# Loads, masks, units and means of a gated-convolution and MLP kernel put in another order

## The chip, the cores and the metric

The kernel runs on one core of one Trainium2 chip. The metric is the time of one execution on the device in microseconds (us). Traces come from the hardware profiler, one execution each. The engines are TensorE (PE for matmuls, PEld for its weight loads), VectorE (DVE), ScalarE (ACT) and GpSimd (POOL); SyncE (SP) issues most DMAs, and ACT's queue issues some.

## What is computed

```python
def _A_ref(q, k, v, shift_k, ssm_k, ssm_D):      # q = layernorm(x)
    ...
        k_shift = k_shift + k_pad[:, t:t + S, :] * shift_k[:, ks - 1 - t][None, None, :]
    kv = k_shift * v
    ...  # FFTs of length L = 2 * S along the sequence
    y_f = kv_f * kf_f[None, :, :, :]
    y = (irfft2 of y_f).astype(jnp.bfloat16)[:, 0, :S, :]
    y = y + kv * ssm_D[None, None, :]
    return q * y

x = A_q
h = x + _A_ref(_layernorm(x, axis=-1), A_k, A_v, A_shift_k, A_ssm_k, A_ssm_D)
h2 = h + _B_ref(_layernorm(h, axis=-1), B_w1, B_w2)     # relu(h @ w1) @ w2
```

S is 2048, D is 512, the shift filter has 4 taps, the MLP is 1376 wide, inputs are bf16. So: four taps along the sequence give kv, a causal convolution as long as the sequence (with ssm_k, one filter per channel) gives y, the gate multiplies it by the normalised x, and an MLP follows.

## The kernel before

The convolution is done as a transform in two matmul stages on each side, a product, and an inverse in two stages. No planner orders the work: it is written out by hand, and each engine runs its instructions in the order of the text. A wait is made only for data or for a buffer that must come free.

- **Loads.** ssm_k comes in eight pieces of 256 KB into kfl: group rg (32 partitions) and half d. `load_rows` (L104) issues both halves of a group. SP issues groups 0 and 2 at once; ACT issues wsh (the taps, L126), drow (ssm_D, L127), group 1 (L128), then the two sines of f1f and group 3 (L222). SP goes on with k (`load_k`, DMA transposes, L140), v (`load_v`, L112), the first quarter of x (`load_x0`, into qn0) and w1 (`load_w1`, L154). There are four buffers for k; two of them first hold tables of turns (tb, L138).
- **Tables.** Integer turns (multiply-add, then a bit mask; `_turns`, L182, on DVE) go through a sine on ACT (`_sin`). f1f, 128x64, becomes f1w for stage 1: a bf16 high part and a low part (f1hi, f1lo, L242 to L244), copied by POOL to the quadrants of f1w (`paired`, L253), the rest zero. `spikes` (L248) does the same to drow for drow2. The large table tab has index i (which 16 of the k1) and b; `turns2`, `sines2` and `negated` (POOL, L275) fill it. Second-stage units read its entries 0 to 2 in the K-side; the product also reads entry 3. `inverse_turns` (POOL, L291) prepares the tables of the inverse, and `diagonals` (POOL, L261) makes wdiag, the taps' weights.
- **Stage 1 of ssm_k.** `s1(gb, engs)` (L423, `stage1`, L343), gb from 0 to 7: 32 matmuls, and four that add drow2, into two PSUM tiles, then two copies to a1k by the engines named ("AD" is ACT and DVE). All PSUM tiles are of two banks; there are four, in two pools taken in turn (`bank2`, L322).
- **Taps.** `tap(u, eng)`, u from 0 to 7: 16 matmuls, one PSUM tile, one copy to ksh.
- **Second-stage units.** `second_k(kp, eng)` (L396), kp from 0 to 15: 8 matmuls from tab and a1k, one PSUM tile, one copy back into a1k.
- **Rows.** `row(q)` (L466, `to_rows`, L329): 16 transposes of ksh by PE, then DVE multiplies by v into xfl. x is normalised on the way: bn_stats, `moments` (L444), `norm_rows` (L451, DVE).
- **Stage 1 of x.** Eight blocks of `stage1` on xfl into a1x (L547). After blocks 0 and 2 stand `column_means` (L404, PE and an ACT copy) and `center` (L412, POOL, 2 of 4 each), which take the column means off w1.
- **Products.** `product(kp, pool)` (L571), kp from 0 to 15: u2 and u1, 8 matmuls and one PSUM tile each; DVE multiplies u2 by a1k into a1x; u1's product goes to DVE, or by an ACT copy (usb) to POOL for ten of the sixteen. `steps` adds three ACT table operations (`last_table`).
- Behind them come the inverse (DVE transposes, L619), the gate, and the MLP with the output. None of that is edited.

Of the kernel before, what the change touches and what calls it, by code (L numbers as in the profile page):

```python
# [9 lines left out]
ALU = mybir.AluOpType  # L10
BF16 = mybir.dt.bfloat16
F32 = mybir.dt.float32
# [3 lines left out]
P = 128  # L16
# [39 lines left out]
def kernel(  # L56
# [37 lines left out]
    def first_channel(rg, d):  # L94
        return 128 * rg + 64 * (d ^ (rg % 2))
# [5 lines left out]

    kfl = front.tile([P, 64, 2, 64], BF16, name="kfl")

    def load_rows(eng, rg):  # L104
        for d in range(2):
            src = bass.AP(tensor=A_ssm_k.tensor, offset=A_ssm_k.offset + S * first_channel(rg, d), ap=[[64, 32], [S, 64], [1, 64]])
            eng.dma_start(out=kfl[32 * rg:32 * rg + 32, :, d, :], in_=src)


    vfl = front.tile([P, 64, P], BF16, name="vfl")  # L110

    def load_v(r):  # L112
        for d in range(2) if r % 2 else (0,):
            n = 64 if r % 2 else P
            src = bass.AP(tensor=A_v.tensor, offset=A_v.offset + first_channel(r, d), ap=[[64 * D, 32], [D, 64], [1, n]])
            nc.sync.dma_start(out=vfl[32 * r:32 * r + 32, :, 64 * d:64 * d + n], in_=src)

    zero = consts.tile([P, 512], BF16, name="zero")
    nc.vector.memset(zero[:], 0.0)
# [2 lines left out]
    nc.vector.memset(drow[:], 0.0)  # L122

    drow2 = consts.tile([P, 2, 64], BF16, name="drow2")
    nc.vector.memset(drow2[:], 0.0)
    nc.scalar.dma_start(out=wsh[:], in_=A_shift_k.rearrange("(r p) j -> p r j", p=P))  # L126
    nc.scalar.dma_start(out=drow[0:P:16, :], in_=A_ssm_D.rearrange("(r g) -> r g", g=64))  # L127
    load_rows(nc.scalar, 1)  # L128
    for rg in (0, 2):
        load_rows(nc.sync, rg)  # L130
    CH = 512
    kT = {}

    def chunk(name):
        return front.tile([P, DC, CH + 16], BF16, tag="kT", name=name, bufs=4)


    tb = [chunk(f"tb{b}")[:].rearrange("p c t -> p (c t)").bitcast(I32)[:, 0:1024].rearrange("p (a b) -> p a b", b=64) for b in range(2)]  # L138

    def load_k(c):  # L140
        kT[c] = chunk("kT")
        if c == 0:
            nc.vector.memset(kT[c][:, :, 0:16], 0.0)
            nc.sync.dma_start_transpose(out=kT[c][:, :, 16:CH + 16], in_=k_d[0:CH, :])
        else:
            nc.sync.dma_start_transpose(out=kT[c][:], in_=k_d[CH * c - 16:CH * c + CH, :])
# [30 lines left out]
    def _sin(out, turns, M, neg=False):  # L177

        nc.scalar.activation(out=out, in_=turns, func=ACT.Sin, scale=(-TURN if neg else TURN) / M,
                             bias=(pbias if neg else nbias)[:])  # L180

    def _turns(out, r, col, M, add):  # L182

        nc.vector.tensor_scalar(out=out, in0=r, scalar1=col, scalar2=add, op0=ALU.mult, op1=ALU.add)
        nc.vector.tensor_single_scalar(out=out, in_=out, scalar=M - 1, op=ALU.bitwise_and)
# [33 lines left out]
    f1f = early.tile([P, 64], F32, name="f1f")  # L219
    _sin(f1f[:, 0:32], t1[:, 0:32], 128)  # L220
    _sin(f1f[:, 32:64], t1[:, 32:64], 128, neg=True)
    load_rows(nc.scalar, 3)  # L222
    o2 = consts.tile([P, 2, 2], F32, name="o2")
    for i in range(2):
        for b in range(2):
            nc.vector.tensor_scalar(out=o2[:, i, b:b + 1], in0=n2c[:], scalar1=32.0 * i, scalar2=4096.0 + 2048.0 * b,
                                    op0=ALU.mult, op1=ALU.add)

    def turns2(i, b):
        ta = tb[b] if i else early.tile([P, 16, 64], I32, tag="ta", name="ta", bufs=2)[:]  # L230
        _turns(ta, r2, n2c[:], 8192, o2[:, i, b:b + 1])
        return ta

    ta00 = turns2(0, 0)
    ta01 = turns2(0, 1)
    f1hi = consts.tile([P, 64], BF16, name="f1hi")
    f1lo = consts.tile([P, 64], BF16, name="f1lo")
    f1d = early.tile([P, 64], F32, name="f1d")


    tab = tabp.tile([P, 32, 4, 64], F32R, name="tab")
    nc.vector.tensor_copy(out=f1hi[:], in_=f1f[:])  # L242
    nc.vector.tensor_tensor(out=f1d[:], in0=f1f[:], in1=f1hi[:], op=ALU.subtract)
    nc.vector.tensor_copy(out=f1lo[:], in_=f1d[:])  # L244

    f1w = consts.tile([P, 2, 2, 64], BF16, name="f1w")

    def spikes():  # L248
        for rg in range(DC):
            q = slice(32 * rg, 32 * rg + 32)  # L250
            nc.vector.tensor_copy(out=drow2[q, rg % 2, :], in_=drow[q, :])  # L251

    def paired():  # L253
        nc.gpsimd.memset(f1w[:], 0.0)
        for rg in range(DC):
            for i, f in enumerate((f1hi, f1lo)):
                nc.gpsimd.tensor_copy(out=f1w[32 * rg:32 * rg + 32, i, rg % 2, :], in_=f[32 * rg:32 * rg + 32, :])  # L257

    wdiag = rows.tile([P, DC, KS, 64], BF16, name="wdiag")

    def diagonals():  # L261
        ident2 = early.tile([P, 64], BF16, name="ident2")
        for e in range(2):
            p = slice(64 * e, 64 * e + 64)
            nc.gpsimd.tensor_copy(out=ident2[p, :], in_=ident[p, p])
        for w in range(DC):
            nc.gpsimd.tensor_tensor(out=wdiag[:, w, :, :], in0=ident2[:].unsqueeze(1).to_broadcast([P, KS, 64]),
                                    in1=wsh[:, w, :].unsqueeze(2).to_broadcast([P, KS, 64]), op=ALU.mult)

    wm = rows.tile([P, 4, 344], F32, name="wm")  # L270

    def sines2(i, b, ta):
        _sin(tab[:, 16 * i:16 * i + 16, b, :], ta, 8192)

    def negated(i):  # L275
        nc.gpsimd.tensor_single_scalar(out=tab[:, 8 * i:8 * i + 8, 2:4, :], in_=tab[:, 8 * i:8 * i + 8, 0:2, :].bitcast(F32),
                                       scalar=-1.0, op=ALU.mult)


# [116 lines left out]
    def second_k(kp, eng):  # L396
        ps = bank2("ps2k")
        second(ps, a1k, kp, 0)
        copy(eng, spot(a1k, kp), ps[:])
# [12 lines left out]
    def center(n):  # L412
        fs = slice(n * FS, (n + 1) * FS)
        nc.gpsimd.tensor_tensor(out=w1[:, :, fs], in0=w1[:, :, fs], in1=wm[:, n, :].unsqueeze(1).to_broadcast([P, DC, FS]),  # L414
                                op=ALU.subtract)


    def warm(n, data=zero[:], lhsT=None):
        ps = bank2("warm")
        for i in range(n):  # L420
            nc.tensor.matmul(out=ps[:, i % 2, :], lhsT=data[:, 0:P] if lhsT is None else lhsT, rhs=data, start=True, stop=True)  # L421
# [26 lines left out]
        nc.gpsimd.tensor_single_scalar(out=r[:, ts, :], in_=mv[:, ts, 1:2], scalar=EPS, op=ALU.add)  # L448
        nc.gpsimd.tensor_tensor(out=r[:, ts, :], in0=r[:, ts, :], in1=mhalf[:, 0:4].unsqueeze(2), op=ALU.pow)

    def norm_rows(q, out, src):  # L451
        for i in range(4):
            t = 4 * q + i
            nc.vector.tensor_scalar(out=out[:, i, :], in0=src[:, i, :], scalar1=mv1[:, t, 0:1],
                                    scalar2=rstd1[:, t, :], op0=ALU.subtract, op1=ALU.mult)

    xfl = None
# [14 lines left out]
    def seconds(kps, engs):  # L472
        for kp, eng in zip(kps, engs):
            second_k(kp, eng)

    load_k(0)
    load_k(1)
    spikes()
    sines2(0, 0, ta00)
    ta10 = turns2(1, 0)  # L480
    sines2(0, 1, ta01)
    ta11 = turns2(1, 1)
    diagonals()
    paired()
    negated(0)
    negated(1)
    sines2(1, 0, ta10)
    sines2(1, 1, ta11)
    load_k(2)
    load_k(3)  # L490
    load_v(0)
    load_v(2)
    load_x0()
    load_v(1)
    load_v(3)
    load_w1()
    negated(2)
    negated(3)
    inverse_turns()
    warm(13, lhsT=wdiag[:, 0, 0:2].rearrange("p j g -> p (j g)"))  # L500
    s1(0, "AD")
    s1(1, "AD")
    s1(2, "AD")
    tap(0, "A")
    s1(3, "AD")
    s1(4, "AD")
    tap(1, "D")
    s1(5, "AD")
    s1(6, "AD")
    s1(7, "AD")  # L510
    tap(2, "A")
    second_k(0, "A")
    second_k(1, "D")
    second_k(2, "A")
    tap(3, "A")
    second_k(3, "D")
    second_k(4, "A")
    tap(4, "A")
    second_k(5, "D")
    pairs_pool()  # L520
    second_k(6, "A")
    tap(5, "D")
    nc.vector.bn_stats(out=st[:, 0, :], in_=qn0[:, 0, :])
    second_k(7, "A")
    tap(6, "A")
    nc.vector.bn_stats(out=st[:, 1, :], in_=qn0[:, 1, :])
    second_k(8, "A")
    tap(7, "D")
    nc.vector.bn_stats(out=st[:, 2, :], in_=qn0[:, 2, :])
    nc.vector.bn_stats(out=st[:, 3, :], in_=qn0[:, 3, :])  # L530
    moments(mv1, rstd1, 0)
    second_k(9, "A")
    row(0)
    second_k(10, "D")
    norm_rows(0, qn0, qn0)
    second_k(11, "A")
    row(1)
    second_k(12, "A")
    row(2)
    second_k(13, "D")  # L540
    second_k(14, "A")
    row(3)
    second_k(15, "A")
    pl.pop("front")
    a1xp = pl.push("a1xp")
    a1x = a1xp.tile([P, 2, 32, 256], F32R, name="a1x")
    for gb in range(8):  # L547
        stage1(lambda g: xfl[:, g // 4, :, :, g % 4], a1x, gb, ("DA", "AD", "AD", "AD", "AA", "AD", "AD", "AD")[gb])
        if gb == 0:
            column_means(0)  # L550
            for n in (0, 1):
                center(n)
        if gb == 2:
            column_means(1)
            for n in (2, 3):
                center(n)
    pl.pop("xp", "rows")

    late = pl.push("late")
# [11 lines left out]
    def product(kp, pool):  # L571
# [13 lines left out]
        (nc.gpsimd if pool else nc.vector).tensor_tensor(out=kk, in0=(usb if pool else u1)[:], in1=kk.bitcast(F32), op=ALU.mult)  # L585

    steps = {
        4: (lambda: last_table(0),),
        7: (lambda: last_table(1),),
        10: (lambda: last_table(2),),  # L590
    }
    for step in steps.get(-1, ()):
        step()
# [262 lines left out]
```

## Time and profile before

| what | us |
|---|---|
| median of 3 runs (202.98 to 300.08) | 203.06 |
| the profiled execution | 203.05 |
| its span, first to last instruction | 201.3 |
| PE busy in the span | 172.1 |
| DVE busy | 147.5 |
| ACT busy | 98.0 |
| POOL busy | 90.7 |
| stage 1 of ssm_k begins (chain of waits) | 14.90 |
| first second-stage unit | 28.46 |
| first row | 40.16 |
| stage 1 of x begins | 50.99 |
| first product | 64.39 |
| inverse begins | 92.37 |
| first full run of the MLP's matmuls | 117.81 |

Times inside the span count from its start. The chain of waits is the work that ended last, followed back from the last instruction; each piece gives its start, its length and the engine and line. "issue" is time in which the engine waited for nothing that the profile shows, such as a DMA's landing. A row of the windows gives each engine's busy time in a stretch, with its number of instructions, and then the granted TensorE clock, the mean busy share of the DMA engines and GB/s.

### The profile page before, as it was taken

How to read it: one execution, taken by the hardware profiler on the slowest of the kernel's cores; microseconds unless marked ns; L12 is line 12 of the kernel's file. 1: busy time of each engine (PE TensorE's matmuls, PEld its weight loads, DVE VectorE, ACT ScalarE, POOL GpSimd, SP SyncE). 2: the span in 40 equal slices, each digit the busy share in tenths (PEclk: the TensorE clock that was granted, in tenths of full speed). 3: DMA queues.
4: the chain of work that ended last, by engine and by line, in shares of the span. 5: the costliest groups of instructions: out<-in, count | busy, mean ns of one | idle time of the engine just before them, and what ended most of it. 6: DMA issues, size and time to landing. Idle time of an engine off the chain costs nothing.

```text
span 201.3 us, 4078 instructions
## 1 busy us (share of the span) xinstructions
PE 172.1 (86%) x1638; PEld 109.2 (54%) x1643; DVE 147.5 (73%) x259; ACT 98.0 (49%) x112; POOL 90.7 (45%) x108
## 2 busy tenths in 40 slices
PE   0369989899896877778967999999999999999992
PEld 0127866498775666656745654545454444444451
DVE  7957866999557999999999779979977580471142
ACT  0387688924786566522985568102630174026300
POOL 7999983120299699991985720220130011002000
PEclk9999999999999999999999999999999999999999
DMA  8999999960000000005902540312420272120022
GB/s 118 216 233 200 212 205 145 187 146 0 3 3 3 0 5 0 0 3 160 235 22 52 154 129 11 61 37 61 101 47 19 61 83 50 38 54 13 3 54 52
DMA packets 51379, 15.99 MB, mean 79 GB/s; under 512 B 46784, under 2 KB 50208, under 8 KB 51360
## 3 DMA queue, kind: packets, MB, share of 16 engines
q1 hardware_dynamic: 42464, 14.61, 35.8%
q10 hardware_dynamic: 8896, 1.12, 3.6%
q8 instruction: 13, 0.21, 0.4%
q14 instruction: 6, 0.05, 0.1%
HBM read 9.64 MB, written 2.10 MB: 58 GB/s over the span
## 4 chain that ended last, share of the span: by engine, by line
PE 67%; DVE 18%; POOL 4%; ACT 4%; issue 3%; ACTq 2%; DVEq 0%; POOLq 0%
PE m L726 19%; PE m L781 18%; DVE a1x L580 7%; PE ps L358 5%; DVE zs L619 5%; PE ps2k L388 4%; PE u L388 4%; PE pkv L375 3%; PE pst L333 3%; DVE a1k L585 3%; ACT a1x L317 3%; PE pz L646 3%; PE pi L614 2%; PE pz L656 2%; POOL f1w L257 2%
## 5 line engine op out<-in xcount | busy, mean ns | idle before, releaser
L762 ACT ACTIVATE h1T<-m 128x512 bf16<-128x512 f32 (+1 forms) x44 | 25.9, 598 | 43.5 <-PE m L726 43.5
L726 PE MATMUL m<-hT,w 128*128 128x512 bf16 (+1 forms) x176 | 39.0, 379 | 0.2 <-ACT hT L693 0.2
L781 PE MATMUL m<-w,h1T 128*128 128x512 bf16 (+1 forms) x161 | 36.1, 379 | 0.2
L787 DVE SCALAR_TENSOR_TENSOR o<-m,rstd,hp 128x128 bf16<-128x128 f32 (+1 forms) x48 | 15.8, 388 | 25.7 <-PE m L781 24.9
L448 POOL TENSOR_SCALAR rstd<-mv 128x4 f32<-128x4 f32 x8 | 1.8, 231 | 64.4 <-DVE mv L446 64.4
L726 PEld LDWEIGHTS <-w 128*128 128x128 bf16 (+1 forms) x176 | 17.4, 100 | 20.4 <-issue 0.5
L781 PEld LDWEIGHTS <-h1T 128*128 128x128 bf16 (+1 forms) x165 | 16.0, 98 | 19.3 <-issue 0.3
L388 PE MATMUL u<-a1x,tab 64*128 64x256 f32 x256 | 19.7, 291 | 6.4 <-DVE a1k L585 2.4
L585 POOL TENSOR_TENSOR a1k<-usb,a1k 128x1024 fp32r<-128x1024 f32 x10 | 23.7, 2393 | 2.3 <-DVE a1x L580 2.2
L627 ACT CAST a1x<-zs 128x1024 fp32r<-128x1024 f32 (+2 forms) x10 | 17.3, 1730 | 11.1 <-DVE zs L619 11.1
L388 PEld LDWEIGHTS u<-a1x,tab 64*128 64x128 f32 x256 | 16.4, 185 | 9.7 <-DVE a1x L580 4.2
L580 DVE TENSOR_TENSOR a1x<-u,a1k 128x1024 fp32r<-128x1024 f32 x16 | 19.1, 1218 | 2.2 <-PE u L388 2.2
L625 POOL CAST a1x<-zs 128x1024 fp32r<-128x1024 f32 (+1 forms) x8 | 15.7, 1969 | 7.4 <-DVE zs L619 7.4
L619 DVE STREAM_TRANSPOSE zs<-pi 128x1024 f32<-128x1024 f32 x16 | 18.4, 1215 | 0.5 <-PE pi L614 0.5
L414 POOL TENSOR_TENSOR w<-w,wm 128x1376 bf16<-128x1376 bf16 x4 | 11.2, 2844 | 11.3 <-ACT wm L410 11.3
L614 PE MATMUL pi<-a1k,wd 128*128 128x512 f32 x32 | 13.3, 417 | 2.6 <-DVE zs L619 1.5
L579 ACT COPY usb<-u 128x1024 f32<-128x1024 f32 x10 | 10.1, 1016 | 10.3 <-PE u L388 10.3
L317 ACT CAST a1k<-ps2k 128x1024 fp32r<-128x1024 f32 x11 | 11.0, 1027 | 7.1 <-PE ps2k L388 7.0
L614 PE MATMUL pi<-a1x,wd 128*128 128x512 f32 x32 | 12.8, 400 | 0.0
L319 DVE CAST a1k<-ps 128x1024 fp32r<-128x1024 f32 x8 | 9.6, 1222 | 4.4 <-PE ps L358 4.4
L319 DVE CAST a1x<-ps 128x1024 fp32r<-128x1024 f32 x7 | 8.4, 1222 | 5.1 <-PE ps L358 5.1
L421 PE MATMUL warm<-zero,wdiag 128*128 128x512 bf16 x13 | 4.5, 518 | 8.4 <-DVE drow L251 8.4
(116 smaller groups left out, 281.1 us busy)
## 6 DMA issues: line engine op xcount, KB each, us to landing
xall<-in_A_q_dram SPq DMA_DIRECT2D x16, 128.0 KB, 3.3
out_dram<-o SPq DMA_DIRECT2D x62, 32.0 KB, 1.6
w<-in_B_w_dram SPq DMA_DIRECT2D x4, 344.0 KB, 6.1
w<-in_B_w_dram SPq DMA_DIRECT2D x1, 1280.0 KB, 7.7
kfl<-in_A_ssm_k_dram SPq DMA_DIRECT2D x4, 256.0 KB, 5.6
kfl<-in_A_ssm_k_dram ACTq DMA_DIRECT2D x4, 256.0 KB, 6.7
vfl<-in_A_v_dram SPq DMA_DIRECT2D x2, 512.0 KB, 6.7
vfl<-in_A_v_dram SPq DMA_DIRECT2D x4, 256.0 KB, 5.4
```

The source lines that it names most:

```text
L317: nc.scalar.copy(out=o, in_=i)
L319: nc.vector.tensor_copy(out=o, in_=i)
L388: nc.tensor.matmul(out=ps[:, d, 256 * i:256 * i + 256], lhsT=tab[rw, k1, b:b + 2, :].rearrange("p b k -> p (b k)"), rhs=a_in[rw, c, k1, :] ...
L580: nc.vector.tensor_tensor(out=spot(a1x, kp), in0=u2[:], in1=kk.bitcast(F32), op=ALU.mult)
L585: (nc.gpsimd if pool else nc.vector).tensor_tensor(out=kk, in0=(usb if pool else u1)[:], in1=kk.bitcast(F32), op=ALU.mult)
L614: nc.tensor.matmul(out=ps[:, b, :], lhsT=wd[:, m:m + 2, :].rearrange("p b k -> p (b k)"), rhs=src[:, d, 16 * b:16 * b + 16, c0:c0 + 32], s ...
L619: nc.vector.transpose(out=zs[:], in_=ps[:].rearrange("p b (k c) -> p c (b k)", c=32))
L627: nc.scalar.copy(out=o, in_=i)
L726: nc.tensor.matmul(out=ps1[:fsz].rearrange("p (i t) -> p i t", i=4), lhsT=w1[:, c, fc * P:fc * P + fsz], rhs=hT[sc][:, c // 2, :, c % 2, : ...
L762: nc.scalar.activation(out=h1T[:fsz, fc, :], in_=ps1[:fsz], func=ACT.Relu)
L781: nc.tensor.matmul(out=ps2[:], lhsT=lhsT, rhs=w2[:ksz, fc, :], start=(fc == 0), stop=(fc == NFC - 1))
L787: nc.vector.scalar_tensor_tensor(out=of(o[:], d)[:, a], in0=ps[:, a], scalar=rstd2[:, t, :], in1=pair(hp[sc][:, d, i, :])[:, a], op0=ALU.m ...
```

## The change

- `load_rows` and `load_v` take the queue and the half. ACT now begins with half 1 of group 1, then drow, then half 0; group 3 has its half 1 first, then wsh, then half 0. SP issues half by half as before.
- turns live in one tile tt of two slots, in place of ta and tb. The first k1 half is made on DVE as before (0,0 ahead of f1w, 0,1 behind it); the second half's multiply-add goes to POOL and only its bit mask (`masked`) to DVE, inside stage 1 and behind unit 0.
- f1w comes from f1f by two masks (ones in the quadrants of one parity): two DVE multiplies, two DVE multiply-subtracts. drow2 comes from drow by the same masks.
- `negated` is split by b: the b = 0 halves stand where both stood, the b = 1 halves behind `moments`.
- POOL's order: inverse_turns and diagonals first, then the table; `norm_rows(0)` moves from DVE to POOL.
- 14 warm-ups on f1w in place of 13 on wdiag.
- taps 1 and 2 go behind stage 1; engines of the copies change; units 12 to 15 go into the product's steps 2, 5, 8 and 11.
- `column_means` and `center` go ahead of stage 1 of x.

```diff
-    nc.vector.memset(drow2[:], 0.0)
-    nc.scalar.dma_start(out=wsh[:], in_=A_shift_k.rearrange("(r p) j -> p r j", p=P))
+    load_rows(nc.scalar, 1, 1)
+    load_rows(nc.sync, 0, 0)
     nc.scalar.dma_start(out=drow[0:P:16, :], in_=A_ssm_D.rearrange("(r g) -> r g", g=64))
-    load_rows(nc.scalar, 1)
-    for rg in (0, 2):
-        load_rows(nc.sync, rg)
+    load_rows(nc.sync, 0, 1)
+    load_rows(nc.scalar, 1, 0)
+    load_rows(nc.sync, 2, 0)
+    load_rows(nc.sync, 2, 1)
...
-    load_rows(nc.scalar, 3)
+    load_rows(nc.scalar, 3, 1)
+    nc.scalar.dma_start(out=wsh[:], in_=A_shift_k.rearrange("(r p) j -> p r j", p=P))
+    load_rows(nc.scalar, 3, 0)
...
+    tt = early.tile([P, 2, 16, 64], I32, name="tt")
+
     def turns2(i, b):
-        ta = tb[b] if i else early.tile([P, 16, 64], I32, tag="ta", name="ta", bufs=2)[:]
-        _turns(ta, r2, n2c[:], 8192, o2[:, i, b:b + 1])
-        return ta
+        t = tt[:, b]
+        (nc.gpsimd if i else nc.vector).tensor_scalar(out=t, in0=r2, scalar1=n2c[:], scalar2=o2[:, i, b:b + 1],
+                                                      op0=ALU.mult, op1=ALU.add)
+        if not i:
+            masked(b)
+
+    def masked(b):
+        nc.vector.tensor_single_scalar(out=tt[:, b], in_=tt[:, b], scalar=8191, op=ALU.bitwise_and)
...
+    def paired():
+        for r in range(2):
+            nc.vector.tensor_scalar(out=f1w[:, 0, r, :], in0=f1f[:], scalar1=mask[:, r:r + 1], scalar2=None, op0=ALU.mult)
+        for r in range(2):
+            nc.vector.scalar_tensor_tensor(out=f1w[:, 1, r, :], in0=f1f[:], scalar=mask[:, r:r + 1], in1=f1w[:, 0, r, :],
+                                           op0=ALU.mult, op1=ALU.subtract)
+
     def spikes():
-        for rg in range(DC):
-            q = slice(32 * rg, 32 * rg + 32)
-            nc.vector.tensor_copy(out=drow2[q, rg % 2, :], in_=drow[q, :])
-
-    def paired():
-        nc.gpsimd.memset(f1w[:], 0.0)
-        for rg in range(DC):
-            for i, f in enumerate((f1hi, f1lo)):
-                nc.gpsimd.tensor_copy(out=f1w[32 * rg:32 * rg + 32, i, rg % 2, :], in_=f[32 * rg:32 * rg + 32, :])
+        for r in range(2):
+            nc.vector.tensor_scalar(out=drow2[:, r, :], in0=drow[:], scalar1=mask[:, r:r + 1], scalar2=None, op0=ALU.mult)
```

The order of the work after the change, from the warm-up to the products (names as above):

```python
    inverse_turns()
    diagonals()
    negated(0, 0)
    negated(1, 0)
    turns2(1, 0)
    warm(14, lhsT=f1w[:, 0].rearrange("p r c -> p (r c)"))
    sines2(0, 1)
    # s1 0, 1 "AD"; turns2(1, 1); s1 2, 3 "AD", 4 "DA", 5 "AD"; tap 0 "D"; s1 6 "AD"; masked(0); s1 7 "DA"
    # tap 1 "A", tap 2 "D"; unit 0 "A"; sines2(1, 0); masked(1); tap 3 "A"; unit 1 "D"; sines2(1, 1)
    # negated(2, 0), negated(3, 0); unit 2 "A"; tap 4 "D"; unit 3 "A"; tap 5 "A"; unit 4 "D"; unit 5 "A"
    # pairs_pool; tap 6 "A"; unit 6 "D"; tap 7 "A"; units 7 to 10 "A" with bn_stats between them
    moments(mv1, rstd1, 0)
    negated(0, 1)
    negated(1, 1)
    negated(2, 1)
    negated(3, 1)
    norm_rows(0, qn0, qn0, nc.gpsimd)
    # row 0; unit 11 "A"; rows 1, 2, 3
    column_means(0)
    column_means(1)
    for n in (0, 1):
        center(n)
    for n in (2, 3):
        center(n)
    # stage 1 of x, eight blocks; products, with units 12 to 15 "A" behind products 2, 5, 8, 11
```

## The prediction

> **What bounds the kernel now.** I read the windows by stage first, then the chain of waits, then kfl's loads. The profiled execution took 203.05 us, its span is 201.3; the median of the three runs is 203.06, so a sum against the profiled execution stands for it. A measurement of this kernel can tell about 2% from no change: under 199.0 us is faster, over 207.1 slower.
>
> ```profile
> core 0: us, PE busy (x) PEld busy (x) DVE busy (x) ACT busy (x) POOL busy (x), PEclk, DMA share, GB/s
> 0.00:14.87 14.87, 4.84 (x18) 1.79 (x19) 11.42 (x33) 6.08 (x7) 13.12 (x37) 1.00 1.17 188
> 14.87:28.46 13.59, 12.94 (x332) 10.20 (x333) 10.63 (x9) 9.67 (x10) 13.00 (x26) 1.00 1.11 211
> 28.46:40.16 11.70, 10.95 (x161) 7.05 (x161) 8.14 (x10) 10.14 (x12) 3.78 (x9) 1.00 0.90 167
> 40.16:50.99 10.83, 10.03 (x112) 9.18 (x113) 9.97 (x20) 4.24 (x5) 1.27 (x2) 1.00 0.31 69
> 50.99:64.39 13.40, 10.92 (x272) 9.10 (x273) 8.38 (x7) 10.39 (x12) 10.19 (x4) 1.00 0.02 4
> 64.39:92.37 27.98, 21.67 (x263) 17.30 (x264) 25.62 (x23) 13.30 (x13) 24.75 (x11) 1.00 0.01 1
> ```
>
> These are loads and tables, stage 1 of ssm_k, taps with second-stage units, rows with units, stage 1 of x with the column means, and the products. The change moves nothing behind 92.37. PE fills 93-95% of the second to fourth stage; in the products it has 6.3 us to spare, while DVE (25.62 of 27.98) and POOL (24.75) are nearly full. The chain of waits shows where PE stands, and where the means lie:
>
> ```profile
> 13.87 1.02 issue
> 14.90 1.05 PE ps L358 x31
> ...
> 25.74 2.40 DVE a1k L319 x2
> 28.15 0.31 issue
> 28.46 1.70 PE ps2k L388 x24
> ...
> 49.56 1.30 DVE xfl L335 x2
> 50.86 0.14 issue
> 50.99 1.09 PE ps L358 x32
> 52.08 1.27 PE pm L408 x8
> ```
>
> POOL's last copy into f1w ends at 13.86, yet stage 1 runs only from 14.9. The rows of kfl, for ACT's last two loads, say why:
>
> ```profile
> L107 ACTq DMA_DIRECT2D kfl<-in_A_ssm_k_dram x2: 2413/2500/2586, 5.2 to 7.8; - x2
> ...
> DMA to landing us min/median/max: 6.8/6.9/7.0
> ```
>
> The first, issued at 5.15, lands 6.8 later, at 11.95; the second, issued at 7.78, at 14.8. So two things hold stage 1: f1w to 13.86 and the last kfl to 14.8. The change must move both.
>
> **The change, part by part.**
>
> *f1w and the warm-up.* L254 and L257 leave POOL (10.02 to 13.86), the three DVE steps of f1hi, f1d, f1lo go, and DVE makes f1w from f1f and two masks: four small operations at 0.2 to 0.34 (L242, L243, L244), about 1 us. f1f ends at 6.88 in the timeline; ACT's sines come no later, since only drow and two loads are issued ahead of them. So f1w stands at about 7.5. The 14 warm-ups start then and take 4.47 x 14/13 = 4.8, to 12.3. Five mask memsets (0.06 to 0.11 each) end before f1f arrives. The two masked copies for drow2 replace 1.85 us of L251 and end near 8.
>
> *kfl.* ACT's queue now issues rows (1,1) at 0.72, where wsh stood; before, its first load went out at 2.41. In the timeline the rows of one ACT load end 1.6 to 1.8 us before the load ahead of it lands (5.02 to 6.8, 7.74 to 9.3, 10.19 to 11.95), and each lands 4.3 to 4.6 after its own issue ends. So landings follow 2.7 apart: 0.72 + 4.4 = 5.1, then 7.8, 10.5 and 13.2; wsh's 4 KB, now ahead of the last, add 0 to its 0.48 of issue. The bounds: no gain, and even 0.5 lost to wsh (14.87 + 0.48 = 15.35); or all 2.1 MB at the 217 GB/s of the seventh microsecond from 2.0 on, 11.7, which the warm-up's end at 12.3 covers. I take 13.3, nearest to this queue's own rows: 14.87 - 13.3 = 1.6 gained. SP's four loads then share the engines from the start, so kT begins about 1 us later; but kT no longer waits for tb (2.7 us in SP's waits, for ACT), so v, x0 and w1 land no later than now (w1 at 37.8 + 7.1 = 44.9).
>
> A rule weighs against this term. The Trainium skill, DMA: Bandwidth & Descriptors, section on issuing engines not being separate DMA queues, says all issuers share the same 16 engines, and a second issuer saves only the sequencer's time, usually small. By that alone the kfl term would be near zero, and the sum 200.1. The windows of one microsecond show 174 GB/s at 2 to 4 us (SP nearly alone) and 216 once both queues run, so the trace does not bear it out for loads of this shape.
>
> *Stage 1 of ssm_k.* Eight ACT copies at 1.02 and eight DVE copies at 1.22 as before; one tap (DVE) lies among them instead of two, and masked(0) (0.69, L185) goes into DVE's queue ahead of the last copy. DVE: 1.1 of PE first, then 9 x 1.22 + 0.69 = 11.7, so the first unit's matmul can start 12.85 after the stage's begin, against 13.59: 0.7 gained. Behind masked(0) wait the last copy and every unit; it waits for turns2(1,0) on POOL. POOL: free of its constants at 7.2, inverse_turns 7.0 (24.91 to 31.92), diagonals 2.9, two half negations at 2.77/2 each, turns2 at 1.2 (L307): 21.1, needed at 13.3 + 10.85 = 24.1. wdiag stands at 17.1, first tap at 20.6. Both covers have 3 us; POOL later than that would be paid one for one.
>
> *Taps and units.* Count from the first unit. Now row 0 starts 11.7 later. After the change ACT owns, up to the copy that frees row 0's PSUM tile: 0.65 for the first matmuls, nine copies at 1.0 (units 0, 2, 3, 5, 7, taps 3, 5, 6, 7), two sines at 1.14, w3's at 0.46: 12.4. So ACT becomes the bound here, and 0.7 is lost. PE then has four rows (4 x 1.6) and unit 11 (0.6): 19.4, plus both means (1.27 + 1.33): 22.0. DVE's last xfl ends at 20.75, so 1.35 of the means fills the gap that is now 49.56 to 50.99. Stage 1 of x starts at 22.0 against 22.53: 0.5 gained, with the means already done. Moving the four units (4 x 0.57) and norm_rows (4 x 0.41 of DVE) is in this.
>
> *Stage 1 of x.* It lasts 13.40, with 2.60 of means inside; without them the DVE and ACT copies set it: two blocks start-up 2.4, six blocks at about 1.25, one ACT-only block more (0.9), the tail of one copy: 11.4. Gained 2.0.
>
> *The products.* Each of the four units brings 8 matmuls (0.6), one ACT copy (1.02) and one PSUM tile. A period of three products has DVE 4 x 1.22 = 4.9, PE 3 x 1.22 + 0.6 = 4.3, ACT 2 x 1.02 + 1.02 + 1.25 (a table) = 4.3: DVE stays the bound. The tile order turns: u1 of the second product behind a unit waits for the unit's copy. Counted in DVE's period, that copy ends 1.0 to 1.4 before it is needed. No stall is therefore the lower end; the upper end is a unit's whole 0.6 at each, 2.4. I take 0.2, nearer the count.
>
> *POOL ahead of the products.* rstd ends 14.5 after the first unit (40.6), then four half negations 5.6, norm_rows four times, center 4 x 2.84 = 11.4. No row shows norm_rows there; by L307 (1.2 for 1024) one is 0.6, by L276 (2.77 for 1024) 1.4. Center ends at 60.0 to 63.2. POOL's first product needs it at 59.5 + 2.7 = 62.2, and POOL ends 0.9 before DVE. So 0 to 1.0 lost; I take 0.1.
>
> Also from the Trainium skill, GPSIMD Engine Reference, on engine selection: one-input work on POOL runs at roughly line rate, two-input work about twice as slow as on VectorE. By that norm_rows would cost about DVE's 0.41 each, an estimate, and the POOL term would be zero; the sum would be 198.4.
>
> **Sum.** 203.05 - 1.6 - 0.7 - 0.5 - 2.0 + 0.2 + 0.1 = 198.55; I say 198.5.
>
> **Rivals.**
>
> *The loads land no sooner.* The total rate caps them. For it: 216 GB/s is flat from 5 to 10 us. Against it: kT's bytes lie among kfl's, and 174 GB/s earlier. Then 198.5 + 1.6 = 200.1.
>
> *POOL is late* at the products by the upper price and the 0.9 of slack is used: 198.5 + 0.9 = 199.4; with norm_rows dearer than any row, 200.
>
> *Units in the products cost their PE time.* For: PE and DVE hand over to each other once a period (70.71, 71.89, 73.15 in the chain). Then 198.5 + 2.2 = 200.7.
>
> *Slower than before:* the units' ACT copies hold the product's PSUM tiles. At each unit DVE would wait for matmuls, copy and the next u1 in turn, 0.6 + 1.02 + 0.6 = 2.2, four times 9.0: 207.5. It decides once ACT's copy comes more than 1.0 later than I count, behind usb or a table (1.25). ACT's 13.30 of 27.98 speaks against it.
>
> **How the numbers follow.** Chances: forecast 0.60, with its own range 197.3 to 199.7 (kfl 1.0 to either side, 0.2 for the rest); loads no sooner 0.14; POOL late 0.08; units at PE's price 0.11; slower 0.07. Some 0.7 of the forecast's share lies under 199.0: faster 0.43; slower 0.07; the rest, 0.50, within 2%. The range runs from 197.0 to 201.2: it takes in every case but the last and the far tails.
>
> **What would show it.** Right: f1w done near 7.5 and stage 1 at 13 to 13.6; the first second-stage unit near 26; means in front of stage 1 of x, which starts near 48 and lasts about 11.4; products from 59.5 with a period of 4.9 and DVE nearly full; the same 109 us behind them. Wrong: ACT's last kfl past 14.5; DVE waiting for tt from POOL before the last stage 1 copy; more than 1.5 us of PE idle ahead of row 0; POOL reaching its first product after 63; a DVE wait behind each unit.

## The result, and the profile after

The changed kernel takes 209.86 us (median of 4 runs, 209.32 to 210.13) against 202.98 for the kernel before: a ratio of 1.033 (95% interval 1.031 to 1.036). Executions more than 1.5% above the fastest of their kernel, such as one of the kernel before at 300.08 us, are left out of the medians and ratios. The change makes the kernel slower, where 198.5 was forecast and 197.0 to 201.2 given as the range. The profiled execution took 209.97 with a span of 208.2, so the 6.9 us of difference can be followed in the span. First the windows, cut at the same six points of the work as before:

```profile
core 0: us, PE busy (x) PEld busy (x) DVE busy (x) ACT busy (x) POOL busy (x), PEclk, DMA share, GB/s
0.00:17.26 17.26, 6.11 (x19) 2.14 (x19) 6.85 (x32) 4.01 (x5) 13.45 (x54) 0.93 1.42 133
17.26:32.06 14.80, 14.69 (x333) 12.48 (x333) 11.40 (x10) 8.91 (x9) 6.75 (x7) 0.85 1.14 186
32.06:43.79 11.73, 11.42 (x170) 7.47 (x169) 9.26 (x12) 11.11 (x14) 3.64 (x3) 1.00 1.09 158
43.79:56.45 12.66, 10.74 (x91) 8.36 (x90) 6.49 (x14) 4.44 (x5) 11.51 (x9) 0.87 0.57 118
56.45:68.02 11.57, 8.66 (x258) 7.79 (x258) 8.29 (x7) 9.57 (x10) 11.57 (x5) 1.00 0.01 3
68.02:98.41 30.39, 24.46 (x294) 20.43 (x296) 25.77 (x23) 17.15 (x17) 27.55 (x12) 0.94 0.01 2
```

Read the second column against the lengths of before (14.90 to the first matmul of stage 1, then 13.59, 11.70, 10.83, 13.40, 27.98). Stage 1 of ssm_k begins 2.4 later and lasts 1.2 longer; taps and units cost 0.0; rows with the means 1.8; stage 1 of x is the one stage that gained, 1.8 where 2.0 was forecast; the products lost 2.4. Behind them another 0.9 is lost (98.41 to the end of the span is 109.8, before 108.9). The sum is 2.4 + 1.2 + 1.8 - 1.8 + 2.4 + 0.9 = 6.9. Two columns at the right show something new: PEclk under 1.00 in four rows, and in the first row 133 GB/s at a DMA share of 1.42, where before it was 188 GB/s at 1.17. The DMA engines were busier and moved less.

The chain of waits (start, length, what) names what stands at the two places:

```profile
7.83 2.65 ACTq L219
10.52 6.69 DMA kfl<-in_A_ssm_k_dram
17.26 1.89 PE ps L360 x31
...
19.58 1.71 PE ps L360 x32
...
21.71 0.99 PE ps L360 x32
...
32.06 0.69 PE ps2k L390 x8
...
46.22 5.11 POOL tab L278 x4
51.32 0.82 issue
52.14 0.64 POOL qn L456
52.78 1.43 issue
54.21 6.22 POOL qn L456 x3
60.43 11.20 POOL w L416 x4
71.65 1.02 ACT usb L585
```

In front of stage 1 the chain is a kfl load, issued at 10.52 and down at 17.21. Then the same 32 matmuls take 1.89, 1.71 and only at the third block 0.99: PE had stood from 12.5 to 17.2, and in windows of one microsecond its granted clock is 0.50 from 15 to 21 and 1.00 again from 22. (The Trainium skill, TensorE: Matmul & The Clock Gate, Part 1, has the clock halved when the array idles and whole again after some 3.4 us of steady work; the trace agrees with the halving, and here the clock is whole again 4.5 us after PE takes up work, at 21.8.) In the products the chain runs through POOL with hardly a gap: half negations, norm_rows (qn), center (w), and from its last instruction straight to the first usb copy on ACT. The waits say the same (engine, line, who is waited for: us, times, longest):

```profile
ACT usb L585 <- POOL w L416: 4.3, 1, 4.3
...
PE pm L410 <- DMA w<-in_B_w_dram: 1.9, 1, 1.9
```

And the rows of kfl's loads from ACT, against 6.8 to 7.0 for the last two before:

```profile
L106 ACTq DMA_DIRECT2D kfl<-in_A_ssm_k_dram x4: 334/474/3934, 0.7 to 10.5; - x4
...
DMA to landing us min/median/max: 4.4/7.0/10.5
```

One of ACT's issues takes 3.93 us, where the longest before took 2.59, so the queue itself is held up. In between, from 8 to 10 us, the rate is 207 to 217 GB/s, the full one of before; at 4 to 8 and 11 to 15 it is 96 to 119.

### The profile page after: what moved, and what is told of

It is laid out like the page before. It is cut to its first block, busy times and chain, and to the rows that moved or that the text cites. A ratio compares the mean times of both kernels' runs of the same rounds, so it can differ in the third digit from the quotient of the medians.

```text
span 208.2 us, 4080 instructions
## 1 busy us (share of the span) xinstructions
PE 178.5 (86%) x1639; PEld 114.5 (55%) x1644; DVE 141.5 (68%) x254; ACT 99.2 (48%) x114; POOL 99.0 (48%) x109
## 4 chain that ended last, share of the span: by engine, by line
PE 55%; DVE 16%; POOL 13%; issue 7%; ACT 4%; DMA 3%; ACTq 2%; DVEq 0%; POOLq 0%
PE m L736 18%; PE m L791 17%; POOL w L416 5%; DVE a1x L586 5%; DVE zs L629 5%; PE ps L360 4%; PE u L390 4%; POOL qn L456 3%; DMA kfl<-in_A_ssm_k_dram 3%; PE pz L656 3%; POOL tab L278 2%; PE pkv L377 2%; DVE a1k L591 2%; PE pz L666 2%; PE ps2k L390 2%
## 5 line engine op out<-in xcount | busy, mean ns | idle before, releaser
L791 PEld LDWEIGHTS <-h1T 128*128 128x128 bf16 (+1 forms) x165 | 15.9, 98 | 19.4 <-issue 0.3
L637 ACT CAST a1x<-zs 128x1024 fp32r<-128x1024 f32 (+2 forms) x10 | 17.2, 1718 | 11.8 <-DVE zs L629 11.8
L390 PEld LDWEIGHTS u<-a1x,tab 64*128 64x128 f32 x256 | 17.4, 195 | 8.1 <-PE u L390 2.4
L278 POOL TENSOR_SCALAR tab<-tab 128x512 fp32r<-128x512 f32 x8 | 11.9, 1517 | 11.1 <-ACT tab L175 11.0
L624 PE MATMUL pi<-a1k,wd 128*128 128x512 f32 x32 | 13.9, 434 | 1.9 <-DVE zs L629 0.8
L360 PE MATMUL ps<-f1w,kfl 64*128 64x128 bf16 x256 | 11.3, 241 | 4.8 <-DMA kfl<-in_A_ssm_k_dram 4.8
L319 ACT CAST a1k<-ps2k 128x1024 fp32r<-128x1024 f32 x13 | 12.8, 1039 | 1.6 <-PE ps2k L390 1.6
L624 PE MATMUL pi<-a1x,wd 128*128 128x512 f32 x32 | 13.2, 412 | 0.0
```

Of the source, the lines that this page charges most:

```text
L360: nc.tensor.matmul(out=pss[h][:, gi // 4, P * (gi % 4):P * (gi % 4) + P], lhsT=data(8 * gb + gi)[rw].rearrange("p d n -> p (d n)"), rhs=f1 ...
L390: nc.tensor.matmul(out=ps[:, d, 256 * i:256 * i + 256], lhsT=tab[rw, k1, b:b + 2, :].rearrange("p b k -> p (b k)"), rhs=a_in[rw, c, k1, :] ...
L624: nc.tensor.matmul(out=ps[:, b, :], lhsT=wd[:, m:m + 2, :].rearrange("p b k -> p (b k)"), rhs=src[:, d, 16 * b:16 * b + 16, c0:c0 + 32], s ...
L637: nc.scalar.copy(out=o, in_=i)
L791: nc.tensor.matmul(out=ps2[:], lhsT=lhsT, rhs=w2[:ksz, fc, :], start=(fc == 0), stop=(fc == NFC - 1))
```

## The experiments

Two questions: why kfl's loads became slow, and what the late center costs. For the first there were two theories. *Queues*: the new order of the loads (ACT's half 1 first, drow among them, both queues at once) slows them. *Place*: the diff also drops f1hi and f1lo (128 bytes a partition each) and adds mask (8 bytes, in a slot of 32). In the memory layout of the built programs wd, w1, kfl and vfl, allocated behind them, lie 224 bytes lower: kfl starts at 40192 (157 x 256) before and at 39968 (156 x 256 + 32) after. Since tb is gone, k's buffers and ksh also change places; they start at a multiple of 256 or 128 past one before, and 32 or 160 past one after. All ratios are to the kernel before on the same chip, with 95% intervals.

**The loads in the order of before.** The changed kernel, with the issue order of the kernel before:

```diff
+    nc.scalar.dma_start(out=wsh[:], ...)
+    nc.scalar.dma_start(out=drow[0:P:16, :], ...)
+    load_rows(nc.scalar, 1, 0)
     load_rows(nc.scalar, 1, 1)
...
-    load_rows(nc.scalar, 1, 0)
...
+    load_rows(nc.scalar, 3, 0)
     load_rows(nc.scalar, 3, 1)
-    nc.scalar.dma_start(out=wsh[:], ...)
-    load_rows(nc.scalar, 3, 0)
```

> The changed kernel with the ssm_k, drow and wsh loads in the order of before; all else changed. Theory LOADS (in the changed kernel the two queues fell to 110 GB/s at 4 to 8 us and again at 10 to 15 us, so the last kfl landed at 17.2 instead of 14.8, PE's clock dropped while it stood, and w1 came at 52.7): last kfl at 14.8 again, stage 1 at 14.9 at full clock, first second-stage unit near 27.8, w1 landed by 46. Theory POOL beside it (norm_rows at 2.07 each on POOL and center behind it, and the first usb copy waits for center): center ends near 67.5, the first usb copy at 67.5 though stage 1 of x ends near 61.5, total near 205. Rival (POOL is late only because the loads were): the first usb copy right behind the first product's matmuls near 62.5, total near 200. Rival to LOADS (the loads' order is not what slowed them): kfl past 16, total 208 to 210.

Measured: 212.87, ratio 1.046 (1.043 to 1.048), slower still. The last kfl was issued at 8.98 and came down 11.25 later, at 20.2; 109 GB/s at 10 to 12 us. With the order of before the slow stretches are still there, so the queues theory falls.

**Only ACT's halves put back** (1,0 before 1,1 and 3,0 before 3,1):

> The changed kernel with ACT's halves in the old order (half 0 of a group first), both queues still begin together and drow and wsh stand where the change put them. If the swapped halves slow the loads: 200 GB/s and more from 3 us on, last kfl by 14, total near 205. If two queues that begin in step slow each other whatever the half, or the small pieces do: 110 GB/s stretches again, kfl near 17, total 209 to 210.

Measured: 210.03, 1.032 (1.029 to 1.035); the last kfl down at 17.3. Here the swap is worth nothing.

**The small loads first** (wsh and drow ahead of all of ACT's rows, halves swapped):

> The changed kernel with wsh and drow ahead of ACT's large loads, as before, and the halves still swapped. If drow and wsh between the large loads slow both queues: no stretch at 110 GB/s, last kfl near 14.8, total near 205. If the swapped halves do: 110 GB/s stretches stay, kfl past 16, total 208 to 210. If the common start does: ACT's first large load again starts at 2.4, so kfl near 14.8 too; e2 parts these two.

Measured: 213.16, 1.049 (1.043 to 1.055); the last kfl down at 19.4. What stands ahead of ACT's rows delays them, as in the first experiment; it does not make the stretches slow.

**norm_rows back on DVE**, all else as changed:

```diff
-    norm_rows(0, qn0, qn0, nc.gpsimd)
+    norm_rows(0, qn0, qn0)
```

> The changed kernel with norm_rows of the first quarter back on DVE; loads as changed. Theory POOL: POOL is free at 52.1, center runs from about 55.5, when its means are there, to 66.7, and the first usb copy no longer waits: 2.4 less in the products, total near 207.4. Rival (POOL's norm_rows was hidden; the products wait for something else): total stays at 209 to 210.

Measured: 205.6, 1.010 (1.007 to 1.013). Center runs from 54.7 to 66.0, the first product's matmuls start at 66.54, and usb no longer waits for center. That took away more than the 2.4 of the products. The dip of the clock behind them is gone too (0.83 from 110 to 120 us in the changed kernel, 1.00 in the same work here). So is PE's wait of 1.9 for w1 ahead of the means, since PE comes to the means later here (52.3 instead of 50.4), and with it the dip in the means (2.75 for them instead of 3.75).

**kfl back at its place.** The changed kernel with mask widened to 256 bytes, two columns of it used; not one instruction works on other data:

```diff
-    mask = consts.tile([P, 2], F32, name="mask")
-    nc.vector.memset(mask[:], 0.0)
+    mask = consts.tile([P, 64], F32, name="mask")
+    nc.vector.memset(mask[:, 0:2], 0.0)
```

> The changed kernel with the mask tile given 256 bytes a partition instead of 8, of which only the old 8 are used. The change took f1hi and f1lo (256 bytes) out of the constants and put mask in (32 with rounding), so kfl, vfl, the k buffers and w1 begin 224 bytes lower than before, at 32 past a multiple of 256 where kfl stood on a multiple; the pad puts kfl back at 40192. Theory ADDRESS (loads of 128-byte pieces are slowed by where they land): no stretch near 110 GB/s in the first 15 us, last kfl by 13.8, stage 1 at full clock, w1 landed by 46. POOL's chain stays (norm_rows 8.3, center 11.2): center ends and the first usb copy comes near 65.8, total near 203. Rival QUEUES (both queues in step, or something that the engines do early, slows the loads): 110 GB/s stretches stay, total 209 to 210.

Measured: 203.3, 0.998 (0.995 to 1.001). From 2 to 10 us the rate is 215 to 217; the last kfl is issued at 8.32 and down at 12.39. From 1.033 to 0.998 is 7.2 us of the 203 of the kernel before. The chain of waits, and the rows of the windows for rows with means and for the products:

```profile
8.32 4.07 DMA kfl<-in_A_ssm_k_dram
12.43 1.06 PE ps L360 x31
...
47.56 6.19 POOL qn L456 x3
53.75 11.18 POOL w L416 x4
64.95 1.02 ACT usb L585
```

```profile
37.16:48.48 11.32, 9.27 (x91) 7.85 (x90) 6.36 (x14) 4.42 (x5) 10.17 (x8) 1.00 0.69 150
...
60.05:91.84 31.79, 24.22 (x294) 20.51 (x296) 25.61 (x23) 17.11 (x17) 28.52 (x12) 0.95 0.01 2
```

Stage 1 has its gain, but the products still take 31.79 where they took 27.98 before, and usb waits 5.5 for center. Ahead of the means PE waits 2.1 for w1, so this wait does not come from the place.

**The kernel before, moved by 32 bytes**: only hsc, one of the last small tiles in front of w1 and kfl, made 32 bytes wider.

```diff
-    hsc = consts.tile([P, 2], F32, name="hsc")
-    nc.gpsimd.memset(hsc[:], 0.0)
+    hsc = consts.tile([P, 10], F32, name="hsc")
+    nc.gpsimd.memset(hsc[:, 0:2], 0.0)
```

> The kernel before with nothing changed but 32 more bytes a partition in the constants (hsc given 10 columns, 2 used), so that kfl, vfl, the k buffers and w1 begin 32 bytes higher, at 32 past a multiple of 256. Theory ADDRESS: stretches near 110 GB/s as in the changed kernel, last kfl past 16.5, stage 1 of ssm_k partly at half clock, total 207 to 213. Rival QUEUES: no difference, 203.

Measured: 209.7, 1.032 (1.026 to 1.037); 132 GB/s at 4 to 6 and 119 at 8 to 13, the last kfl down at 18.9, first unit at 33.9 instead of 28.5. None of the change is in this kernel. Place decides.

**Which multiple, and which tile.** The same with 64 and with 128 bytes, then with gaps around kfl: kfl alone 32 past, and all of the others 32 past with kfl at a multiple of 256.

```diff
+    gap1 = front.tile([P, 8], F32, name="gap1")
+    nc.gpsimd.memset(gap1[:], 0.0)
     kfl = front.tile([P, 64, 2, 64], BF16, name="kfl")
...
+    gap2 = front.tile([P, 56], F32, name="gap2")
+    nc.gpsimd.memset(gap2[:], 0.0)
     vfl = front.tile([P, 64, P], BF16, name="vfl")
```

> The kernel before, with hsc widened by 64 bytes a partition: kfl starts at 40256, 64 past a multiple of 256, and vfl, w1, k's buffers and everything behind them move by 64 as well. It asks how far from which multiple a start must lie to be slow. If what counts is a multiple of 64 (a 128-byte piece then fills whole lines of 64): 203.5, 215 GB/s flat from 5 to 10 us, ACT's last kfl down at 14.8. If what counts is a multiple of 128 or of 256: as with 32 bytes, 210, under 135 GB/s at 4 to 6 and at 8 to 13 us, the last kfl down near 19.

> The same with 128 bytes: kfl starts at 40320, 128 past a multiple of 256. If 64 or 128 is what counts: 203.5 and 215 GB/s. If 256 is what counts: 210. If the shift itself did harm, by which tile lies where and not by the start's remainder (the rival): slow in both of these runs.

> The kernel before with a gap of 32 bytes in front of kfl and one of 224 behind it, so that kfl alone starts 32 bytes past a multiple of 256 (40224), and vfl, w1, k's buffers and ksh keep their remainders. If ssm_k's own writes, in pieces of 128 bytes, are what slows: the last kfl down near 19 and about 209 to 210. If it is k's transposed loads: the last kfl at 14.8 and 203.5. If both share it: between, 206.

> The other half of it: kfl at a multiple of 256 (40448), and vfl, w1, k's buffers and ksh 32 bytes past one. If ssm_k's writes are what slows: 203.5 to 204, the last kfl down at 14.8. If it is k's loads, which run beside the last kfl from about 8 us: the last kfl down near 19 and 209 to 210, 110 GB/s at 8 to 13 us, and no slow stretch at 4 to 6. If both share it: between, 206.

Measured, in this order: ratios 1.028 (1.024 to 1.032), 0.999 (0.997 to 1.001), 1.028 (1.024 to 1.031), 0.999 (0.996 to 1.002). 64 past is as slow as 32, 128 past costs nothing, kfl alone makes the loss, and vfl, w1 and k's buffers 32 past a multiple of 256 make none. So it is the writes of ssm_k's 128-byte pieces. A multiple of 128 is quick; that leaves two readings: no piece may lie over a boundary of 128, or none over one of 256 (half 0 of kfl begins each 256 bytes, half 1 lies 128 behind, so at 32 past only half 1's pieces lie over a boundary of 256). To part them, kfl alone 160 past, with gaps of 160 and 96 bytes in the same way:

> The kernel before with gaps of 160 and 96 bytes around kfl, so that kfl alone moves, to 40352, 160 past a multiple of 256. A piece of half 0 starts at kfl's start plus a multiple of 256, a piece of half 1 128 bytes behind it. With 32 or 64 past, a piece of half 1 lies over a boundary of 256 bytes and one of half 0 does not; with 160 it is the other way round; with either, every piece lies over a boundary of 128. If a boundary of 256 is what counts, the slow stretches change places: SP's first load, half 0 of group 0, runs nearly alone from 2 to 3.5 us and went at 168 to 173 GB/s with 32 past; now it falls to 110 to 130, and one of the slow stretches of 32 past (4 to 6, 9 to 13) becomes quicker; the time is again 208 to 210. If a boundary of 128 is what counts, the windows are as with 32 past: 170 from 2 to 4, 145 from 4 to 6, 110 from 9 to 13, and 209.

Measured: 209.26, 1.029 (1.027 to 1.031). The windows with kfl 32 past, then 160 past (the last two columns are DMA share and GB/s):

```profile
2.00:4.00 2.00, 0.00 (x0) 0.00 (x0) 1.79 (x10) 0.00 (x0) 1.81 (x5) 1.00 1.25 171
...
11.00:13.00 2.00, 2.00 (x6) 0.73 (x5) 1.97 (x3) 0.00 (x0) 1.93 (x3) 1.00 1.72 109
```

```profile
2.00:4.00 2.00, 0.00 (x0) 0.00 (x0) 1.79 (x10) 0.00 (x0) 1.81 (x5) 1.00 1.45 143
...
11.00:13.00 2.00, 2.00 (x6) 0.76 (x5) 1.96 (x3) 0.00 (x0) 1.96 (x3) 1.00 1.39 216
```

The stretch at 11 to 13 goes from 109 to the full 216, and the first load, quick with 32 past, is slow with 160: 96 to 133 GB/s from 3 to 4 us (168 to 178 with 32 past), though not yet in the microsecond before it, which was expected slow as well. The stretches have changed places, which the boundary of 256 foretells and the boundary of 128 does not.

**Both mended**: mask widened, and norm_rows on DVE.

> The changed kernel with the pad, and norm_rows of the first quarter on DVE. If ADDRESS and POOL's chain are all that went wrong, this is what the prediction summed up: stage 1 at 13.3, first unit at 26.2, stage 1 of x at 48, products at 59.5, total 198.5 to 199.5. Rival (another wait takes their place: ACT ahead of row 0, DVE's norm_rows, the units in the products): 201 or more, and the trace names it.

Measured: 198.76, ratio 0.975 (0.971 to 0.979). It beats both kernels. Its windows:

```profile
0.00:12.46 12.46, 4.95 (x19) 1.84 (x19) 6.75 (x32) 4.00 (x5) 10.19 (x49) 1.00 1.17 183
12.46:25.44 12.98, 12.84 (x332) 10.42 (x333) 11.28 (x10) 8.88 (x9) 9.91 (x12) 1.00 1.09 194
25.44:37.21 11.77, 11.46 (x172) 7.50 (x169) 9.24 (x12) 11.12 (x14) 3.64 (x3) 1.00 0.97 178
37.21:47.44 10.23, 9.49 (x91) 7.95 (x90) 8.25 (x18) 4.43 (x5) 7.57 (x7) 1.00 0.64 143
47.44:59.01 11.57, 8.66 (x259) 7.80 (x258) 8.29 (x7) 9.55 (x10) 11.02 (x4) 1.00 0.01 3
59.01:87.41 28.40, 23.02 (x294) 19.21 (x296) 25.61 (x23) 17.11 (x17) 23.73 (x10) 1.00 0.01 2
```

and the part of its chain that leads to the products:

```profile
38.57 6.67 DMA w<-in_B_w_dram
...
45.29 1.06 PE pm L410 x6
...
47.19 11.27 POOL w L416 x4
58.47 0.54 issue
59.01 1.22 PE u L390 x16
```

The clock is whole in every row. The chain runs through center, which ends at 58.47, but the product does not wait for it: with the wide mask alone it starts at 60.05 while center runs on to 64.95. DVE's last a1x copy ends at 58.8, and the product reads a1x. In both kernels it starts 0.2 behind that copy (59.84 with the wide mask alone), so the copy sets 59.01. Center is needed by the first usb copy, at 60.32, and is covered by 1.85 us; w1's landing at 45.24, from which the means and center follow, could come that much later.

**The load order alone**: this best version with the load order of before (the first diff above).

> As e6_pad_norm, with the ssm_k, drow and wsh loads in the order of before. What the new order of the loads is worth by itself, at good addresses: kfl's last at 14.8 against 13.3 or so, so 1.5 later from stage 1 on: total near 200.2. Rival (the total rate caps the loads, the order is worth nothing): equal to e6_pad_norm within 0.5.

Measured: 200.57, 0.984 (0.981 to 0.987); the last kfl down at 14.6 and stage 1 at 14.68, against 12.39 and 12.46. The new order is worth 2.2 us at the begin of stage 1 and 1.8 in the medians. ACT's first rows go out at 0.72 instead of 2.41, and from 2 to 4 us the rate is 213 to 216 GB/s instead of 176 to 183. With the order of before the last kfl is even issued sooner (7.7 instead of 8.4), and takes 6.9 to land instead of 4.0; which of the swaps in the order makes this the run does not tell. (By the rule of the Trainium skill that the prediction weighed, DMA: Bandwidth & Descriptors, "Issuing engines are not separate DMA queues", a second issuing engine saves only the sequencer's time, usually small. Both versions issue from two engines, so the rule itself is not tried; what the order saves here is not small.)

## Why the prediction was wrong

**The step that failed first is "kfl"**, and with it the sentence that each load "lands 4.3 to 4.6 after its own issue ends", taken from rows of before. At kfl's new place that price does not hold: the last load lands 6.2 after its issue ends. The forecast was worked out edit by edit, and no edit touches kfl; but dropping two small tiles and adding one moves it, and the durations taken from the trace of before were carried to a place where they do not hold. Predicted -1.6, measured +2.4, of which the place makes 4.8 (17.26 against 12.46 or 12.43 with the wide mask). It does not stop there: PE's clock drops while it stands, so stage 1 lost 1.2 in place of gaining 0.7, and in the means the clock is at half too (it is whole there with kfl at its place), which makes 1.0 of the 1.8 that "rows and means" lost.

**The step that failed second is "POOL ahead of the products"**, in both halves. norm_rows was bounded by 0.6 and 1.4 from POOL's integer and fp32 rows of 1024 elements; the groups of the changed kernel have

```profile
L416 POOL TENSOR_TENSOR w<-w,wm 128x1376 bf16<-128x1376 bf16 x4 | 11.2, 2864 | 0.0
...
L456 POOL TENSOR_SCALAR qn<-qn,mv,rstd 128x512 bf16<-128x512 bf16 x4 | 8.3, 2103 | 0.0
L456 DVE TENSOR_SCALAR qln<-xall,mv,rstd 128x512 bf16<-128x512 bf16 x12 | 4.1, 410 | 4.4 <-POOL rstd L451 4.4
```

2.10 for 512 elements on POOL and 0.41 for the same operation on DVE: 8.3 us in all, 2.7 above the upper bound of 5.6. Of the rows it was bounded by, L307 has the two per-partition operands but int32 data, and L276 has a constant in their place and fp32 data. The prediction's estimate from the Trainium skill (GPSIMD Engine Reference, 4.1 Engine selection: one-input work at roughly line rate), by which it would have been DVE's 0.41, is off by a factor of five here.

The other half is the due time. The prediction took center to be needed by POOL's first product, at 59.5 + 2.7. It is needed earlier, by ACT's first usb copy: center reads wm, which lies at 125536 to 131040 in the pool rows, and the three buffers of usb (118016 to 130304 before) take over memory of the pools that are given up in front of the products, rows among them. In the built programs of before and after, the first usb copy does carry a wait for center's last instruction, and the trace of the changed kernel shows it. That memory is the reason is read from the layout and was not tried by itself (the first copy's own buffer, 118016 to 122112, does not lie over wm). With kfl at its place the first product starts at 60.05, so usb's matmuls were done at 61.35; center ends and usb starts at 64.95. Of these 3.6 us, 2.75 are center's end past the 62.2 allowed and 0.85 the earlier due time. With norm_rows on DVE as well, usb starts at 60.32 and waits for nothing but its matmuls, and the products take 28.40 instead of 31.79. The trace of before had it in plain view: center ended at 65.44, the first usb copy started at 65.71, a cover of 0.27 that was never priced.

**A smaller step failed beside it**: "w1 land no later than now", at 44.9, with which rows and means were to take 22.0 from the first unit. With kfl at its place and norm_rows on POOL PE is at the means from 43.8 and waits 2.1 for w1's last piece, which is issued at 39.6 and down at 46.2, and the stretch takes 23.04 (25.44 to 48.48). With norm_rows on DVE the rows end later, w1 is down at 45.24 and the stretch takes 22.0. Why w1 comes 1.0 later in the one than in the other no run shows. The 3.4 of the products and this 1.0 are nearly all of the 4.55 by which the two medians differ (203.31 - 198.76).

**What held.** With the two put right, the sum came out, stage by stage (forecast, then measured on the mended kernel against the span of before): loads -1.6 and -2.4 (ACT's loads land at 4.8, 7.2, 9.7 and 12.4, where 5.1, 7.8, 10.5 and 13.2 were forecast); stage 1 of ssm_k -0.7 and -0.6; taps, units and rows -0.5 and -0.5, at 22.0 after the first unit as forecast (25.44 to 47.44); stage 1 of x -2.0 and -1.8; the products +0.3 and +0.4, DVE the bound at 25.61 of 28.40, with a period of 5.0; behind them 0 and 0.0 (108.9). That is -5.0 in the span (201.3 to 196.3), against -4.5 in the forecast. That it comes so near is in part luck: the loads gained 0.8 more than forecast, which covers 0.4 lost on the other terms. Nor is this the kernel that was forecast, since norm_rows is back on DVE; the forecast change with kfl at its place stands at 203.3.

**The rivals.** "The loads land no sooner" and "units in the products cost their PE time" are refuted on the mended kernel. "POOL is late" was the right mechanism at a third of its price: up to 200, 1.5 above the forecast, with norm_rows dearer than any row, while 4.55 was paid with kfl at its place. The rival on the slower side, units' copies holding PSUM tiles, gave nearly the time that came, 207.5 (four times 2.2 is 8.8, so 207.3), by a mechanism that is not there: no DVE wait of 2.2 behind each unit, but one wait of 4.3 at the first usb copy, and 4.8 before stage 1. Its chance of 0.07 stood for the wrong thing; what was missing is a rival in which the layout moves.

**The two causes add up** in the ratios to the kernel before, which take out the difference between chips: the place is worth 7.2 us with norm_rows on POOL (1.033 to 0.998) and 7.1 with it on DVE (1.010 to 0.975), norm_rows 4.8 at the bad place and 4.7 at the good one.

## What to carry to other kernels

A change that drops, adds or resizes a small tile moves every tile allocated behind it, so list the start addresses of the DMA destinations before and after, and for a load in pieces of 128 bytes, as here, keep each piece inside a block of 256. Durations from a trace hold for the layout they were taken in. When work is moved to another engine, find its price from a row of the same operation, types and operands, and look for the first reader or the next owner of its memory, not only for the next instruction on its engine.

## What the hardware showed that was not expected

- The rate of a DMA into the core's memory depended on where the destination starts: 216 GB/s with the 128-byte pieces inside blocks of 256 bytes, 108 to 119 in the stretches where they lie over a boundary, with the DMA engines busier (share 1.38 and 1.7). 32 bytes of shift cost 3.2% of this kernel. The Trainium skill has the nearest rule in DMA: Bandwidth & Descriptors, "How a descriptor splits into AXI transactions": transactions start from multiples of 256 bytes, a start off them costs extra. It tells this of reads; for the writes here the traces agree as to pieces over a boundary. That a piece at 128 past costs more, which the rule would give, does not show: in the kernel before all pieces of half 1 lie 128 past and all of half 0 at a multiple, and from 5 to 10 us the rate is a flat 216 to 217 GB/s for both.
- How long PE stands does not by itself tell whether its clock drops. In the changed kernel it dropped to 0.50 in a stand of 4.8 us, and also in one of 1.9 ahead of the means; with kfl at its place it stayed at 1.00 through a stand of 2.05 at the same spot and dropped in one of 2.6 in the products. Stands of 1.6 (before) and 1.4 (the mended kernel with the old load order) did no harm. Once dropped, it was whole again 3.0 us after PE took up work (those products) at the soonest and 5.9 (stage 1 with norm_rows on DVE) at the latest of the cases read.
- Center on POOL took 2.86 for each quarter (1376 elements, two inputs), norm_rows 2.10 (512 elements, one input and two per-partition scalars): 2.1 ns and 4.1 ns an element, so the operation with fewer inputs was the dearer.
